# Linear-attention and gated-MLP block on one core: other queues for the first loads, a row-tiled spread of 1/den, and new instruction orders

## The chip, the core and the metric

The kernel runs on one core of a Trainium2 chip. The metric is the device time of one execution in microseconds (us); smaller is better. Three runs of the kernel before gave a median of 241.5 us, from 240.93 to 242.02. One more execution was profiled. Times inside the profile count from the start of its span.

## The reference

Two blocks follow each other on x, which has 2048 tokens and 512 features. All data is bf16.

```python
# A: linear attention, 32 heads of 16
q, k, v = split(layernorm(x) @ wqkv)
phi = lambda t: where(t > 0, t + 1, exp(t)) + 1e-6
pq, pk = phi(q), phi(k)
kv, z = einsum('bhsd,bhse->bhde', pk, v), einsum('bhsd->bhd', pk)
num, den = einsum('bhqd,bhde->bhqe', pq, kv), einsum('bhqd,bhd->bhq', pq, z) + 1e-6
h = x + merge_heads(num / den) @ wo
# B: gated MLP with a mix over tokens, Fh = 896
zz = gelu(layernorm(h) @ w_in)
z1, z2 = zz[..., :Fh], layernorm(zz[..., Fh:])
g = einsum('ts,bsf->btf', w_sp, z2) + b_sp
out = h + (z1 * g) @ w_out
```

## The kernel before, in words

Tokens are worked in 16 tiles of 128 (n = 0 to 15), which form 4 groups of 512 (gq or tg = 0 to 3). In the order of the work:

- **Loads** (L495, called from L507 to L520). The x tiles 0, 2 and 3 and then wq (the query weights) go out on SP's DMA queue, x tile 1 and then wk (the key weights, 512 KB) on ScalarE's. An x tile is 128 KB. SP goes on with the other x tiles.
- **First layernorm, per tile**: statistics on VectorE (L576, then L580, here "stats" and "aggr"), 1/sqrt of the variance on ScalarE as Ln and Exp (L590, L592) for tiles 0 to 3, then the normalisation on VectorE (L611, "norm"). Tiles 0 to 3 are transposed by TensorE (L645, "tr": four matmuls) and copied from PSUM by ScalarE (L652, "copy"); the others go through DMA transposes on SP's queue (L637).
- **Key projection** (L734, "k0" is that of tile 0, four matmuls) and its phi on ScalarE and VectorE (L711 to L720); products of keys and normalised x (L766); **query projection** (L748), which needs the transposes of all four tiles of its group.
- **The denominator**, for two groups of tokens at a time (`den`, L849): a matmul in four column strips (L858), Ln and Exp on ScalarE for the reciprocal (L863, L866), a spread over heads and features by matmuls with the 0/1 matrix `sel` (L874, four 128x128 matmuls per group, one PSUM bank), a copy on ScalarE per group (L878), and two multiplications of pq by it on VectorE per group (L882, each a half of the group's tokens).
- The product of kv and wo (L819, L829, L838, its copies L845 and L847), the attention output (L904, four matmuls per tile) added to x on VectorE (L909), the second layernorm (L576 again, L618), DMA transposes, then the two halves of the first MLP matmul (L939, L970), the token mix (L1009) and the last projection (L1027).

Ahead of the real work, and between its first pieces, TensorE runs matmuls on constants whose results nobody reads (L564, "dummies"). Eight stand at the start, two wait for the first stats, one for the first Exp; four short ones follow tr0 and tr1.

Nothing is scheduled at run time. Every operation of the program has a number, counted in the order in which the Python code makes it. `ORDER` lists the numbers; each engine executes its own operations in that order and waits on semaphores for what they need. An operation that waits holds up everything behind it on its engine. `SLOT` gives each PSUM or SBUF tile its place.

The order of `ORDER` at the start of the kernel before reads, engine by engine:

- SP: x0, x2, x3, wq, x4-5, ... ; ScalarE: x1, wk, table load, Ln0, Exp0, Ln2, Exp2, copy0, Ln1, Exp1, copy2, ...
- VectorE: stats0, aggr0, stats2, norm0, aggr2, stats1, norm2, aggr1, stats3, norm1, aggr3, norm3, ...
- TensorE: 8 + 2 dummies, tr0, 3 dummies, tr2, k0, tr1, k2, dummy, tr3, k1, dummy, k3, four query parts, ...

Of the kernel before, what the change touches and what calls it, by code (L numbers as in the profile page):

```python
# [7 lines left out]
ACT = mybir.ActivationFunctionType  # L8
ALU = mybir.AluOpType

P = 128
# [1 line left out]


ORDER = [
# [34 lines left out]
]  # L50
SLOT = [
# [6 lines left out]
]  # L58


# [294 lines left out]
def bass_sequential_preLN__linear_attn_block__mixer_gmlp__prompt_kernel(  # L355
# [11 lines left out]
    _, S, D = A_x.shape  # L367
# [3 lines left out]
    GW = 512  # L371
    NT, KD, KF, NG = S // P, D // P, FH // P, S // GW
    TPG = GW // P
# [101 lines left out]
    def bank(i):  # L475
        return lambda a: a[:, i, :]
# [10 lines left out]
    def act_c(n, ptr=0):  # L487
        return 0.07 + 0.000833 * n + 0.093 * ptr
# [18 lines left out]
        xl[a] = load(eng, f"x{a}", x[a:b, :], x_dram[a * P:b * P, :].rearrange("(n p) d -> p n d", p=P),  # L507
                     int((b - a) * P * D * 2 + more), bias, **kw)

    load_x("sp", 0, 1)  # L510
    load_x("act", 1, 2)
    load("act", "wk", wqkv[:, D:2 * D], w3[:, :, D:2 * D], D * D * 2)
    load_x("sp", 2, 3)
    load_x("sp", 3, 4)
    load("sp", "wq", wqkv[:, 0:D], w3[:, :, 0:D], D * D * 2)
    for a in (4, 6):
# [332 lines left out]
    def den(gs):  # L849
        n = len(gs)  # L850
        t = Tile(PS)
        pq = View(s_tq, (NG + gs[0]) * GB_, [n, KD, GW], BF16)

        def mm(e):
            for c in range(KD):
                for j in range(TPG):
                    o = t(bank(0)).ap()[CG * j:CG * (j + 1), 0:n * P].rearrange("p (g k) -> p g k", g=n)
                    i = e.matmul(o, lhsT=zb.ap[:, CG * c:CG * (c + 1)], rhs=pq.ap[:, :, c, j * P:(j + 1) * P],  # L858
                                 start=(c == 0), stop=(c == KD - 1), skip_group_check=True)
            return i  # L860
        op("pe", n * MM, mm, r=[zb.all(), pq.all()], w=[t()], mode=1)
        rr, rb = rr_v[gs[0]:gs[-1] + 1, :], rb_v[gs[0]:gs[-1] + 1, :]
        op("act", act_c(n * P, 1), lambda e: e.activation(  # L863
            flat(rr.ap()), t(bank(0)).ap()[:, 0:n * P], ACT.Ln, bias=eps[1:2].ap(), scale=1.0),
           r=[t(), eps[1:2]], w=[rr])
        last_lnexp.append(op("act", act_c(n * P), lambda e: e.activation(rb.ap(), rr.ap(), ACT.Exp, scale=-1.0),  # L866
                             r=[rr], w=[rb]))
        for gq in gs:
            t2 = Tile(PS)
            r1, rs = rb_v[gq, :], rs_v[gq, :]  # L870

            def sp_(e, t2=t2, r1=r1):
                for j in range(TPG):
                    k = e.matmul(t2(bank(0)).ap()[:, j * P:(j + 1) * P], lhsT=sel.ap[:, j * P:(j + 1) * P], rhs=r1.ap(),  # L874
                                 start=True, stop=True, skip_group_check=True)
                return k
            op("pe", 4 * MS, sp_, r=[sel.all(), r1], w=[t2()])
            op("act", act_c(GW), lambda e, t2=t2, rs=rs: e.activation(rs.ap(), t2(bank(0)).ap(), ACT.Copy), r=[t2()],  # L878
               w=[rs])
            for a in (0, GW // 2):  # L880
                d, m = pqT[gq][:, a:a + GW // 2], rs_v[gq, a:a + GW // 2]
                op("dve", dve_c(KD * GW // 2, 2), lambda e, d=d, m=m: e.tensor_tensor(  # L882
                    d.ap(), d.ap(), m.ap().rearrange("p (a f) -> p a f", a=1).to_broadcast([P, KD, GW // 2]),
                    ALU.mult), r=[d, m], w=[d])
# [202 lines left out]
```

## Time and profile before

| | |
|---|---|
| median of three runs | 241.5 us |
| profiled execution, its own time | 240.84 us |
| its span in the profile | 239.6 us |
| TensorE busy | 98% of the span |
| VectorE busy | 55% |
| ScalarE busy | 33% |

The profile lists what each engine did and when. A chain of waits is followed back from the last instruction: each piece of it is the work that the next piece waited for. A row of it has the start in us, the length in us, the engine, the tile and the line. In a timeline a matmul's length also has the time in which its result drains, so that consecutive matmuls overlap there; in the chain they don't. In a list of DMA issues the last number is the time from issue to landing.

### The profile page before, as it was taken

Reading aid. Unit: us, or ns where it says so; the run is one execution under the profiler, and the core shown is the slowest. Engines: PE = TensorE matmul, PEld = TensorE weight load, DVE = VectorE, ACT = ScalarE, POOL = GpSimd, SP = SyncE. Lnnn points to the kernel's source line nnn. Section 1 sums busy time; section 2 is a strip of 40 time slices with the busy share of each in tenths; the row PEclk is TensorE's granted clock in tenths of the full one; section 3 lists DMA queues with packets and bytes.
Section 4 is the critical chain, followed back from the end, with each engine's and each line's share of the span. In section 5 each row is a group of like instructions: output and inputs, shape, how many; then the busy total and the mean of one; then the engine's idle time right before and its main releaser. Section 6 shows DMA issues by size and latency. Waiting matters only on the chain.

```text
span 239.6 us, 3023 instructions
## 1 busy us (share of the span) xinstructions
PE 235.2 (98%) x1172; PEld 110.3 (46%) x1194; DVE 132.6 (55%) x269; ACT 79.2 (33%) x101; POOL 34.1 (14%) x84
## 2 busy tenths in 40 slices
PE   8999999999999999999999999999999999999996
PEld 2544444554444454544444444444444444444443
DVE  4898866389999934996233233341333513323444
ACT  3883844784666889654600000000000000000000
POOL 7114312001334600436000000000000000000000
DMA  6941349966232332594444544445000200000022
GB/s 205 320 88 26 74 101 266 351 101 138 71 68 44 68 66 59 130 208 89 91 106 93 88 107 95 102 105 117 0 0 0 68 23 0 0 3 0 0 87 88
DMA packets 56702, 21.83 MB, mean 91 GB/s; under 512 B 50704, under 2 KB 55824, under 8 KB 56688
## 3 DMA queue, kind: packets, MB, share of 16 engines
q1 hardware_dynamic: 54928, 16.62, 31.6%
q0 software_dynamic: 944, 4.33, 5.7%
q10 hardware_dynamic: 816, 0.70, 1.0%
q8 instruction: 9, 0.15, 0.3%
q14 instruction: 5, 0.04, 0.1%
HBM read 7.47 MB, written 2.10 MB: 40 GB/s over the span
## 4 chain that ended last, share of the span: by engine, by line
PE 96%; DMA 1%; issue 1%; DVE 1%; ACT 0%; ACTq 0%
PE ps L1009 40%; PE ps L1027 10%; PE ps L939 10%; PE ps L970 10%; PE ps L766 6%; PE ps L734 6%; PE ps L748 6%; PE ps L904 6%; DMA xh<-in_A_x_dram 1%; PE ps L645 1%; PE ps L858 0%; PE ps L838 0%; PE ps L782 0%; PE ps L874 0%; PE ps L819 0%
## 5 line engine op out<-in xcount | busy, mean ns | idle before, releaser
L1009 PE MATMUL ps<-wsp,pk_xn_z 128*128 128x512 bf16 x328 | 72.6, 379 | 0.4
L1016 DVE TENSOR_TENSOR e<-ps,e 128x512 bf16<-128x512 f32 x28 | 19.3, 691 | 68.1 <-PE ps L1009 68.1
L1009 PEld LDWEIGHTS ps<-wsp,pk_xn_z 128*128 128x128 bf16 x336 | 32.9, 98 | 39.6
L939 PE MATMUL ps<-win,hT 128*128 128x384 bf16 (+1 forms) x126 | 25.9, 352 | 0.1
L970 PE MATMUL ps<-hT,win 128*128 128x512 bf16 x109 | 25.6, 379 | 0.2
L1027 PE MATMUL ps<-wout,xT_pq_z 128*128 128x512 bf16 (+2 forms) x118 | 24.6, 366 | 0.1
L1009 PE MATMUL ps<-wqkv_wsp,pk_xn_z 128*128 128x512 bf16 x110 | 24.2, 379 | 0.1
L576 DVE BATCH_NORM_STATS2 small<-xh 128x6 f32<-128x512 bf16 x32 | 21.0, 676 | 3.5 <-DMA xh<-in_A_x_dram 3.4
L948 DVE BATCH_NORM_STATS2 small<-pk_xn_z 128x6 f32<-128x512 bf16 (+1 forms) x32 | 18.0, 605 | 7.4 <-ACT pk_xn_z L944 7.4
L711 ACT ACTIVATE e<-ps 128x1024 bf16<-128x1024 f32 x16 | 16.4, 1027 | 12.6 <-PE ps L734 8.6
L939 PEld LDWEIGHTS ps<-win,hT 128*128 128x128 bf16 x128 | 12.5, 98 | 12.6
L1027 PEld LDWEIGHTS ps<-wout,xT_pq_z 128*128 128x128 bf16 x119 | 11.5, 98 | 13.0
L1033 DVE TENSOR_TENSOR e<-ps,xh 128x512 bf16<-128x512 f32 (+2 forms) x17 | 11.2, 660 | 11.3 <-PE ps L1027 11.3
L1009 PEld LDWEIGHTS ps<-wqkv_wsp,pk_xn_z 128*128 128x128 bf16 x112 | 10.9, 98 | 13.2
L597 POOL TENSOR_TENSOR small<-small 128x2 f32<-128x2 f32 x22 | 16.6, 764 | 1.5
L970 PEld LDWEIGHTS ps<-hT,win 128*128 128x128 bf16 x112 | 10.9, 98 | 12.5 <-ACT xT_pq_z L975 0.3
L975 ACT ACTIVATE xT_pq_z<-ps 128x1024 bf16<-128x1024 f32 (+1 forms) x16 | 14.1, 917 | 7.5 <-PE ps L970 7.3
L944 ACT ACTIVATE pk_xn_z<-ps 128x896 bf16<-128x896 f32 x16 | 14.4, 916 | 5.7 <-PE ps L939 5.7
L734 PE MATMUL ps<-wqkv_wsp,xT_pq_z 128*128 128x512 bf16 x64 | 15.7, 379 | 0.0
L766 PE MATMUL ps<-pk_xn_z 128*128 128x512 bf16 x62 | 15.5, 379 | 0.2 <-issue 0.2
L748 PE MATMUL ps<-xT_pq_z,wqkv_wsp 128*128 128x512 bf16 x61 | 14.7, 379 | 0.2
L904 PE MATMUL ps<-pk_xn_z,xT_pq_z 128*128 128x512 bf16 x63 | 14.3, 379 | 0.2 <-issue 0.2
(71 smaller groups left out, 172.9 us busy)
## 6 DMA issues: line engine op xcount, KB each, us to landing
out_dram<-e SPq DMA_DIRECT2D x15, 128.0 KB, 1.7
win<-in_B_w_in_dram POOLq DMA_DIRECT2D x1, 1792.0 KB, 9.9
xh<-in_A_x_dram SPq DMA_DIRECT2D x4, 256.0 KB, 6.1
wout<-in_B_w_out_dram POOLq DMA_DIRECT2D x1, 896.0 KB, 6.3
wsp<-in_B_w_sp_dram SPq DMA_TRANSPOSE x48, 2.9
wqkv_wsp<-in_A_wqkv_dram ACTq DMA_DIRECT2D x1, 512.0 KB, 4.9
wqkv_wsp<-in_A_wqkv_dram SPq DMA_DIRECT2D x1, 512.0 KB, 5.6
xh<-in_A_x_dram SPq DMA_DIRECT2D x1, 512.0 KB, 7.2
```

The source lines that it names most:

```text
L576: op("dve", dve_c(512), lambda e: e.bn_stats(s6.ap(), src.ap()), r=[src], w=[s6])
L597: return op("pool", 0.665, lambda e: e.tensor_tensor(dst.ap(), dst.ap(), h.ap(), ALU.pow), r=[dst, h], w=[dst])
L734: i = e.matmul(t(bank(ti)).ap(), lhsT=lhs.ap()[:, c, :], rhs=rhs.ap()[:, c, :], start=(c == 0), stop=(c == KD - 1))
L748: r_ = e.matmul(t(bank(i)).ap(), lhsT=lhs.ap()[:, c, :], rhs=rhs.ap()[:, c, :], start=(c == 0), stop=(c == KD - 1))
L766: r = e.matmul(txk[h](bank(i)).ap(), lhsT=xx.ap()[:, c * P:(c + 1) * P], rhs=kk.ap(), start=(n == 0), stop=(n == NT - 1))
L904: i = e.matmul(t(bank(ti)).ap(), lhsT=l.ap()[:, c, :], rhs=mw[c, :].ap(), start=(c == 0), stop=(c == KD - 1))
L939: k = e.matmul(t(bank(i)).ap()[:, 0:b - a], lhsT=l.ap()[:, c, :], rhs=win[c, a:b].ap(), start=(c == 0), stop=(c == KD - 1))
L948: op("dve", dve_c(b - a), lambda e, s6=s6, src=src: e.bn_stats(s6.ap(), src.ap()), r=[src], w=[s6])
L970: k = e.matmul(t(bank(i)).ap(), lhsT=l.ap()[:, c, :], rhs=r_.ap()[:, c, :], start=(c == 0), stop=(c == KD - 1))
L1009: k = e.matmul(t(bank(0)).ap(), lhsT=l.ap()[:, s - a, :], rhs=r_.ap()[:, s - a, :], start=(s == 0), stop=(s == NT - 1))
L1016: op("dve", dve_c(512), lambda e: e.tensor_tensor(gb().ap(), t(bank(0)).ap(), bsp().ap()[:, tg * GW:(tg + 1) * GW], ALU.add), r=[t(), bsp( ...
L1027: k = e.matmul(t(bank(0)).ap()[:, 0:b - a], lhsT=l.ap()[:, fc, :], rhs=wout[fc, a:b].ap(), start=(fc == 0), stop=(fc == KF - 1))
```

## The change

Four things change.

1. x tile 0 is loaded in two halves of 256 columns, one issued by SP and one by ScalarE. Tiles 1 and 2 follow on ScalarE's queue. wk goes out on SP's queue, second there, ahead of x3 and wq.
2. The spread of 1/den takes one operation for a pair of groups. For each j of 0 to 3 it multiplies only the 32 rows of `sel` and of the reciprocals that matter (rows 32j to 32j+31) and 256 columns, each j into a bank of its own: four matmuls for two groups where there were eight.
3. The copies after it take two banks each and are cut by halves of the tokens (a = 0, 1) in place of groups. The multiplications L882 stay as they were.
4. `ORDER` and `SLOT` are new. The numbers in the new `ORDER` are shifted by one from the second load on.

```diff
 ORDER = [
-    0, 3, 4, 5, 27, 28, 13, 24, 15, 11, 18, 19, 1, 2, 26, 35, 36, 12, 14, 29, 30, 31, 32, 37, 38, 21, 33, 20, 25, 22,
-    23, 49, 39, 50, 34, 123, 124, 40, 125, 126, 127, 51, 42, 6, 7, 8, 9, 10, 52, 41, 53, 43, 17, 56, 44, 54, 45, 46,
...
+    28, 29, 0, 3, 5, 6, 7, 8, 1, 36, 30, 31, 32, 33, 34, 35, 124, 125, 17, 9, 2, 4, 27, 10, 11, 22, 23, 25, 14, 15, 12,
+    24, 16, 19, 13, 26, 43, 37, 44, 20, 38, 21, 50, 39, 40, 45, 46, 51, 47, 52, 126, 41, 127, 53, 42, 48, 54, 128, 129,
...
-    load_x("sp", 0, 1)
+    for i, (eng, a, b) in enumerate((("sp", 0, D // 2), ("act", D // 2, D))):
+        load(eng, f"x0{'ab'[i]}", x[0, a:b], x_dram[0:P, a:b], P * D, BIG)
     load_x("act", 1, 2)
-    load("act", "wk", wqkv[:, D:2 * D], w3[:, :, D:2 * D], D * D * 2)
-    load_x("sp", 2, 3)
+    load("sp", "wk", wqkv[:, D:2 * D], w3[:, :, D:2 * D], D * D * 2)
+    load_x("act", 2, 3)
     load_x("sp", 3, 4)
...
+        t2 = [Tile(PS, 2), Tile(PS, 2)]
+        r1 = rb_v[gs[0]:gs[-1] + 1, :]
+        def spread(e):
+            for j in range(TPG):
+                q = slice(CG * j, CG * (j + 1))
+                k = e.matmul(t2[j // 2](bank(j % 2)).ap()[:, 0:n * P], lhsT=sel.ap[q, j * P:(j + 1) * P], rhs=r1.ap()[q],
+                             start=True, stop=True, skip_group_check=True)
+            return k
+        op("pe", MM * n / TPG, spread, r=[sel.all(), r1], w=[t2[0](), t2[1]()], mode=2)
+        for a in range(2):
+            rs = rs_v[gs[0]:gs[-1] + 1, a * GW // 2:(a + 1) * GW // 2]
+            op("act", act_c(GW), lambda e, t2=t2, rs=rs, a=a: e.activation(
+                rs.ap().rearrange("p g (j t) -> p j g t", j=2),
+                t2[a]().ap()[:, :, 0:n * P].rearrange("p j (g t) -> p j g t", g=n),
+                ACT.Copy), r=[t2[a]()], w=[rs])
         for gq in gs:
-            t2 = Tile(PS)
-            r1, rs = rb_v[gq, :], rs_v[gq, :]
-            def sp_(e, t2=t2, r1=r1):
-                for j in range(TPG):
-                    k = e.matmul(t2(bank(0)).ap()[:, j * P:(j + 1) * P], lhsT=sel.ap[:, j * P:(j + 1) * P], rhs=r1.ap(),
-                                 start=True, stop=True, skip_group_check=True)
-                return k
-            op("pe", 4 * MS, sp_, r=[sel.all(), r1], w=[t2()])
-            op("act", act_c(GW), lambda e, t2=t2, rs=rs: e.activation(rs.ap(), t2(bank(0)).ap(), ACT.Copy), r=[t2()],
-               w=[rs])
```

Read by engine, the new lists say:

- SP: x0 left half, wk, x3, wq, x4-5, ... ; ScalarE: x0 right half, x1, x2, table load, Ln0, Exp0, Ln1, Exp1, Ln2, Exp2, copy0, copy1, Ln3, Exp3, copy2, copy3, ...
- VectorE: stats0, stats1, aggr0, aggr1, stats2, norm0, aggr2, norm1, norm2, stats3, aggr3, norm3, ... (36, 43, 37, 44, 50, 40, 51, 47, 54, ... in the new numbers)
- TensorE: 8 + 2 + 1 dummies, tr0, dummy, tr1, 3 dummies, tr2, k0, k1, tr3, k2, three query parts, k3, the fourth, ... No dummy stands behind k0.
- Later, TensorE: the last two query parts, then L904 for tiles 0, 1, 2, 3, 6, L858 for groups 2 and 3, L904 for tile 4, the spread of groups 2 and 3, tiles 5, 7, 14, 8, 9, 15 and 10 to 13. VectorE multiplies group 0's tokens of tiles 0 and 1 (L882) right after the copy L847. In the kernel before, L904 began with tile 2, and two tiles (6 and 7) stood between L858 and the spread.
- The mix and the last projection keep their order; three L970 blocks move in between the first pieces of the mix.

76 rows, old and new, of tables (ORDER, SLOT) are left out of this document.

## The prediction

> **What bounds the kernel now.** The page comes first, for the share of each engine, then the chain of waits in order of time.
>
> ```profile
> span 239.6 us, 3023 instructions
> PE 235.2 (98%) x1172; PEld 110.3 (46%) x1194; DVE 132.6 (55%) x269; ACT 79.2 (33%) x101; POOL 34.1 (14%) x84
> ```
>
> ```profile
> 3.45 0.71 DVE small L576
> ...
> 4.17 0.19 DVE small L580
> ...
> 5.51 0.61 PE ps L645 x4
> 6.12 0.61 PE ps L564 x3
> 6.73 0.27 PE ps L645 x4
> 7.01 0.86 PE ps L734 x4
> ...
> 9.08 0.22 PE ps L645 x4
> ...
> 10.28 0.86 PE ps L734 x4
> 11.14 0.43 PE ps L748 x2
> ...
> 44.29 0.55 PE ps L858 x16
> ...
> 46.67 0.45 PE ps L874 x8
> ...
> 50.60 0.99 PE ps L838 x16
> 51.59 1.85 PE ps L748 x8
> ...
> 56.90 0.55 PE ps L858 x16
> ...
> 226.01 11.63 PE ps L1027 x60
> ```
>
> From 5.51 us to 237.64 (226.01 + 11.63) TensorE is the chain without a break worth naming. So the time is the start of TensorE's real work, plus its work, plus a tail that the change leaves alone. Three things can move it: when the real work begins and whether it runs on from there; how much TensorE work there is; and stalls that the new orders bring where there are none. The profiled execution took 240.84 us, 1.24 more than its span and 0.66 less than the median of 241.5. The sum is made on 240.84 and its difference is then put on the median.
>
> **The front: a yardstick.** At 11.14 TensorE has done four tr and four k. After the change, by the orders, tr0 to tr2 and all dummies stand ahead of k0; then k0, k1, tr3, k2 and k3 can run back to back with query parts between them. That is four times 0.86 and one tr of 0.22, 3.66 us from the start K of k0. The front gains if K lies before 11.14 - 3.66 = 7.48, counted as the chain counts.
>
> **The front: the loads.** Here are the issues and their landings: tile 0 on SP and tile 1 on ScalarE, then wk on ScalarE, tile 2 on SP, then tile 3 on SP. Two rows of timelines give the issue times, and the last row is all that DMA queues moved from 3.66 to 4.70 us (q10 is ScalarE's queue).
>
> ```profile
> xh<-in_A_x_dram SPq DMA_DIRECT2D x1, 128.0 KB, 2.6
> xh<-in_A_x_dram ACTq DMA_DIRECT2D x1, 128.0 KB, 2.8
> ```
> ```profile
> wqkv_wsp<-in_A_wqkv_dram ACTq DMA_DIRECT2D x1, 512.0 KB, 4.9
> xh<-in_A_x_dram SPq DMA_DIRECT2D x1, 128.0 KB, 2.7
> ```
> ```profile
> xh<-in_A_x_dram SPq DMA_DIRECT2D x1, 128.0 KB, 4.4
> ```
> ```profile
> 0.80 1.33 SPq L495 DMA_DIRECT2D xh<-in_A_x_dram  x3
> ```
> ```profile
> 1.24 0.46 ACTq L495 DMA_DIRECT2D wqkv_wsp<-in_A_wqkv_dram  x1
> ```
> ```profile
> DMA packets 321, 0.33 MB, mean 316 GB/s; under 512 B 0, under 2 KB 321, under 8 KB 321
> ...
> q10 hardware_dynamic: 321, 0.33, 92.2%
> ```
>
> SP's first three issues took 1.33 us together, so they stand some 0.45 apart: 0.80, 1.24, 1.70. Tile 1 landed at 0.80 + 2.8 = 3.6, tile 2 at 1.24 + 2.7 = 3.9, wk at 1.24 + 4.9 = 6.1, tile 3 at 1.70 + 4.4, also 6.1. Tile 3 is the telling one. It was issued on another queue than wk, half a microsecond later, and waited for it: for over 1 us nothing but wk's packets moved. The two queues therefore do not share the rate evenly. A small load issued after wk lands after wk, whichever queue it is on.
>
> The change puts wk second on SP, at 1.24, and tile 1 second on ScalarE, at about the same time; tile 2 comes third, at about 1.70, surely behind wk. Whether tile 1 goes ahead of wk is open. I take the case that wk goes first, since tile 2 and wk were issued together before, at 1.24, and SP's was through first: tile 2 landed at 3.9, while more than half of wk moved after 3.66. Then tile 1 is the end of 768 KB where tile 3 was the end of 1024. At 316 GB/s the 256 KB between are 0.83 us, so tile 1 lands at about 5.3 and tile 2, 0.4 later, at 5.7. Bounds: 3.6 (as before) and 6.1 (as tile 3 before).
>
> The Trainium skill has a rule that would soften this ("DMA: Bandwidth & Descriptors", Queues, rings and completion order): each DMA engine alternates between the queues it has work for, after a packet of typically 9 to 17 descriptors. Tile 1 would then slip in after half of wk, and by an estimate from the rate above land near 4.7. The row of 321 packets, more than half of wk's 512 and with none of SP's among them, speaks against so early a turn.
>
> **The front: who waits for tile 1.** This is what decides. The new VectorE order is stats0, stats1, aggr0, aggr1, stats2, norm0. VectorE executes in order, so aggr0, with tile 0 long ready, stands behind stats1 and its wait for tile 1; and norm0 stands behind stats2. Splitting tile 0 in halves then gains nothing. The steps by the old distances between starts:
>
> ```profile
> 4.17 0.18 DVE L580 BATCH_NORM_AGGREGATE small<-small 128x2 f32<-128x6 f32 x1
> 4.27 0.66 DVE L576 BATCH_NORM_STATS2 small<-xh 128x6 f32<-128x512 bf16 x1
> 5.02 0.43 DVE L611 TENSOR_SCALAR pk_xn_z<-xh,small 128x512 bf16<-128x512 bf16 x1
> 5.38 0.16 DVE L580 BATCH_NORM_AGGREGATE small<-small 128x2 f32<-128x6 f32 x1
> 5.46 0.65 DVE L576 BATCH_NORM_STATS2 small<-xh 128x6 f32<-128x512 bf16 x1
> 6.14 0.41 DVE L611 TENSOR_SCALAR pk_xn_z<-xh,small 128x512 bf16<-128x512 bf16 x1
> ```
> ```profile
> 5.57 0.29 ACT L590 ACTIVATE small<-small 128x1 f32<-128x1 f32 x1 [0.58 <-DVE small L580]
> 5.90 0.20 ACT L592 ACTIVATE small<-small 128x1 f32<-128x1 f32 x1
> 6.16 0.60 ACT L652 ACTIVATE xT_pq_z<-ps 128x512 bf16<-128x512 bf16 x1
> ```
>
> stats1 starts at 5.33; aggr0 0.72 later (3.45 to 4.17), at 6.05; aggr1 0.10 later, stats2 at 6.25 (tile 2 is there); norm0 0.68 later (5.46 to 6.14), at 6.93. aggr2 follows 0.36 later (5.02 to 5.38), at 7.29. Ln2 comes 0.20 after aggr2 (5.38 to 5.57), at 7.49, Exp2 0.33 later at 7.82, norm2 0.24 later (5.90 to 6.14), at 8.06. copy0 stands behind Exp2 on ScalarE and starts at 8.05; tr2 starts 0.49 after norm2 (5.02 to 5.51) and takes 0.22, so TensorE is free for k0 at 8.77, and copy0's 0.60 is over by 8.65. The chain counts a piece up to 0.17 later than the timeline (k0: 7.01 against 6.84 when its first matmul starts). So **K = 8.94**, and the front costs 8.94 - 7.48 = 1.46 us. wk itself (6.1 before, now earlier in the line) is there long before k0. Tile 3 and wq have the same bytes ahead of them as before, and their readers come later. The table load on ScalarE moves by one DMA issue of 0.46 and hides in the wait for Ln0 at 6.25; if tile 1 came at 3.6 it would still be done before Ln0. GpSimd makes its constants in another order, and their first reader, Ln0, comes later too.
>
> **The spread.** Two sets of eight 128x128 matmuls, 0.45 us each (46.67), become two sets of four on 32 rows and 256 columns. The rows of before have no row-tiled matmul. The nearest is L858, tiled in four column strips: 16 matmuls of 256 columns, at 0.108 (half of 0.86 / 4) 1.73 us one by one, took 0.55, so four ran at once, with 0.12 over. By that a set of four takes 0.11 + 0.12 = 0.23, and two sets save 0.44. Bounds: four at once without the 0.12, 0.11 a set, saves 0.68; one by one, 0.55 a set, costs 0.20. I take 0.44. The copies keep their number and size (512 elements each); they lie beside TensorE.
>
> The skill has the same drain as a rule ("TensorEngine Tiling (Array Packing)", Key Properties): a change of tiling mode drains TensorE. Without the drain the sum would be 0.24 lower; the 0.12 in L858 agrees with the rule.
>
> **The new orders behind the front.** TensorE has no wait to lose, so they can only add. Two places are short of cover.
>
> ```profile
> 51.66 1.22 DVE L847 CAST pk_xn_z<-ps 128x1024 bf16<-128x1024 f32 x1
> 52.79 0.68 DVE L882 TENSOR_TENSOR xT_pq_z<-xT_pq_z,wsp 128x1024 bf16<-128x1024 bf16 x1
> ```
> ```profile
> 57.50 0.47 ACT L863 ACTIVATE wsp<-ps,small 128x256 f32<-128x256 f32 x1 [2.08 <-PE ps L858]
> 58.01 0.42 ACT L866 ACTIVATE wsp<-wsp 128x256 bf16<-128x256 f32 x1
> ```
>
> First, L904 now begins with tile 0, which needs the L882 that follows L847. That ended at 53.47 (52.79 + 0.68), while TensorE was free at 53.44 (51.59 + 1.85): a stall of about 0.1 with the hop. Second, from the end of L858 (57.45) to the end of L866 (58.43) are 0.98 us. One L904 tile (0.86) now covers them, where two did: about 0.15. Behind it VectorE's order L909, L882, L909 leaves each L882 some 0.1 of slack by the same rows; a slip there costs up to 0.5. I take 0.25 for all, with 0 and 1.0 as bounds.
>
> **The sum**: +1.46 - 0.44 + 0.25 = +1.27. 240.84 becomes 242.1; on the median, 241.5 becomes **242.8 us**, slower by 0.5%.
>
> **The rivals.**
>
> *Tile 1 goes ahead of wk.* It then lands near 3.7 and stats1 starts at 4.17, but tile 2 still lands behind wk, at 5.7, and norm0 stands behind stats2: norm0 6.41, Exp2 7.30, copy0 7.53, norm2 7.54, k0 at 8.25 + 0.17 = 8.42, the front +0.94. 242.3 us. For it: ScalarE's two issues are short. Against it: SP's turn above.
>
> *Not slower: the loads share after all.* If wk gives way to tiles 1 and 2, so that they land by 4.1 and 4.9, stats1 starts 0.72 after stats0 at 3.45, at 4.17, and K is 8.94 - 1.16 = 7.78; with tile 0's halves 0.3 earlier, 7.5. The front is then 0 to +0.30 and the spread decides: 241.3 to 241.6. The point from which it decides is tile 1 at 4.1, tile 2 at 5.0. Against it: tile 3 before.
>
> *TensorE stays at half pace.* Ten dummies before tr0 went at half pace, and so did tr0:
>
> ```profile
> 0.83 4.42 PE L564 MATMUL ps<-const-bfloat16-1.0 128*128 128x512 bf16 x10 [0.83 <-PEq L1072]
> ```
>
> 0.43 each against 0.22 (0.86 / 4) for later ones of that size. The full pace came after 5.5 us of nearly unbroken dummies. In my forecast they end at 5.3 and the next waits for Exp0, until about 6.6. If the pace is not reached ahead of tr0, three tr at 0.43 and four dummies at 0.21 put k0 at 7.42 + 2.14 + 0.17 = 9.73: 0.8 more, 243.6. The skill's rule ("TensorE: Matmul & The Clock Gate", Part 1) is a free-running window of some 3.4 us that has to be busy; this trace shows one transition only and can't date the window.
>
> *The spread isn't tiled.* The four run one by one: +0.20 in place of -0.44, 243.4.
>
> **How the numbers follow.** The forecast has 0.34, tile 1 ahead of wk 0.24, sharing 0.24, half pace 0.13, the spread untiled 0.05. A difference of 0.5% is about what a measurement of this kernel can tell from no change: above 242.7 is slower, under 240.3 faster. Half pace, the spread and most of the forecast are slower, 0.46. The second case, sharing and the forecast's lower part are the same, 0.46; the low end of sharing with the best spread (0.24 more) and no stall (0.25 more) comes near faster, 0.08. The range runs from 240.8, sharing with those two, to 243.7, half pace.
>
> **What would show it.** Right: stats1 starts after 5 us, released by a DMA, and aggr0 behind it; tr0 begins near 7.4; k0 to k3 have no dummy between them; each spread takes 0.23 in the chain and small waits stand ahead of the first L904 and of the second spread. Wrong: stats1 directly behind stats0; a row of DMA packets in which both queues move while wk is under way; or a wait of TensorE over 0.5 us behind the front, which I have not priced.

## The result and the profile after

The changed kernel takes 245.3 us (median of six executions, 243.86 to 245.72), the kernel before in the same measurement 241.5 (240.91 to 242.02): a ratio of 1.016, 95% interval 1.0137 to 1.0182. It is slower by 3.8 us, where the prediction had 1.3 and a range that ended at 243.7. The profiled execution took 245.30 us, 4.46 more than that of before.

The first two lines of the page, after:

```profile
span 244.0 us, 3008 instructions
PE 237.7 (97%) x1163; PEld 110.7 (45%) x1186; DVE 132.5 (54%) x269; ACT 79.1 (32%) x101; POOL 35.5 (15%) x84
```

TensorE is busy for 2.5 us more than before, with nine instructions fewer. So part of the loss is not waiting: the same work went slower. The chain of waits, after (start, length, what; the lines of the file are shifted: L577 is stats, L612 norm, L646 tr, L565 the dummies, L735 the key projection, L749 the query projection, L859 the denominator, L875 the spread, L910 the attention output):

```profile
1.72 5.08 DMA xh<-in_A_x_dram
...
6.82 0.69 DVE small L577
7.51 0.31 DVE pk_xn_z L612
7.83 0.10 DVE small L581
...
7.97 0.58 PE ps L646 x4
...
8.77 0.43 PE ps L646 x4
...
9.84 0.43 PE ps L646 x4
10.26 3.37 PE ps L735 x8
13.63 0.22 PE ps L646 x4
13.85 0.86 PE ps L735 x4
...
51.14 0.22 PE ps L875 x4
51.36 0.99 PE ps L749 x4
...
63.79 0.29 PE ps L875 x4
64.08 5.29 PE ps L910 x24
...
238.68 3.43 PE ps L1033 x22
```

Three things are to be seen. The chain now begins with the load of tile 2, issued at 1.72 and landed at 6.80, where it began with tile 0. K, the start of k0, is 10.26. And k0 and k1 took 3.37 together, 1.69 each, where a key projection takes 0.86 (the row at 13.85): TensorE ran at half pace until the end of k1, and tr0 to tr2 went at 0.43 and more, not 0.22.

The account by the prediction's yardstick: before, four tr and four k were done at 11.14. After, k0 and k1 (3.37), tr3 (0.22), k2 and k3 (twice 0.86) from 10.26 on make 15.57. The front is 4.43 us later, and the last matmul ends at 242.11 where it ended at 237.64: 4.47 later. **The whole loss is in the front, by 13.63 us, where k1 ends.** All that is behind it, spread and new orders together, comes to nothing.

The timeline of the front, after (in brackets the idle time ahead and what ended it):

```profile
3.03 0.69 DVE L577 BATCH_NORM_STATS2 small<-xh 128x6 f32<-128x512 bf16 x1 [3.03 <-DMA xh<-in_A_x_dram]
5.77 0.69 DVE L577 BATCH_NORM_STATS2 small<-xh 128x6 f32<-128x512 bf16 x1 [2.04 <-DMA xh<-in_A_x_dram]
6.38 0.30 DVE L581 BATCH_NORM_AGGREGATE small<-small 128x2 f32<-128x6 f32 x2
...
7.22 0.61 PE L565 MATMUL ps<-const-bfloat16-1.0 128*128 128x512 bf16 x1 [1.97 <-ACT small L593]
```

Tile 0's halves let stats0 start at 3.03 (3.45 before), and nothing comes of it: stats1 waits for tile 1 until 5.77, aggr0 behind it starts at 6.38, and TensorE stands idle for 1.97 us. The load lists, from issue to landing, for the two issued at 1.24 and for the two at 1.70:

```profile
wqkv_wsp<-in_A_wqkv_dram SPq DMA_DIRECT2D x1, 512.0 KB, 4.8
xh<-in_A_x_dram ACTq DMA_DIRECT2D x1, 128.0 KB, 4.5
```
```profile
xh<-in_A_x_dram SPq DMA_DIRECT2D x1, 128.0 KB, 4.9
xh<-in_A_x_dram ACTq DMA_DIRECT2D x1, 128.0 KB, 5.1
```

Tile 1 needed 4.5 us where before it needed 2.8; tile 2 needed 5.1 where it needed 2.7.

### The profile page after: what moved, and what is told of

It is laid out like the page before. It is cut to its first block, busy times and chain, and to the rows that moved or that the text cites. A ratio compares the mean times of both kernels' runs of the same rounds, so it can differ in the third digit from the quotient of the medians.

```text
span 244.0 us, 3008 instructions
## 1 busy us (share of the span) xinstructions
PE 237.7 (97%) x1163; PEld 110.7 (45%) x1186; DVE 132.5 (54%) x269; ACT 79.1 (32%) x101; POOL 35.5 (15%) x84
## 4 chain that ended last, share of the span: by engine, by line
PE 95%; DMA 2%; issue 1%; DVE 1%; ACT 0%; ACTq 0%
PE ps L1015 39%; PE ps L945 10%; PE ps L1033 10%; PE ps L976 10%; PE ps L735 6%; PE ps L749 6%; PE ps L767 6%; PE ps L910 5%; DMA xh<-in_A_x_dram 2%; PE ps L646 1%; PE ps L859 0%; PE ps L839 0%; PE ps L783 0%; PE ps L820 0%; ACTq L495 0%
## 5 line engine op out<-in xcount | busy, mean ns | idle before, releaser
L945 PE MATMUL ps<-win,hT 128*128 128x512 bf16 (+1 forms) x127 | 25.5, 352 | 0.1
L577 DVE BATCH_NORM_STATS2 small<-xh 128x6 f32<-128x512 bf16 x32 | 21.0, 677 | 5.2 <-DMA xh<-in_A_x_dram 5.1
L1033 PEld LDWEIGHTS ps<-wout,xT_pq_z 128*128 128x128 bf16 x119 | 11.5, 98 | 13.0
L735 PE MATMUL ps<-wqkv_wsp,xT_pq_z 128*128 128x512 bf16 x63 | 17.2, 410 | 0.1
L749 PE MATMUL ps<-xT_pq_z,wqkv_wsp 128*128 128x512 bf16 x61 | 14.9, 380 | 0.2
L910 PE MATMUL ps<-pk_xn_z,xT_pq_z 128*128 128x512 bf16 x62 | 14.2, 379 | 0.1
```

Source lines behind the costliest of these rows:

```text
L577: op("dve", dve_c(512), lambda e: e.bn_stats(s6.ap(), src.ap()), r=[src], w=[s6])
L735: i = e.matmul(t(bank(ti)).ap(), lhsT=lhs.ap()[:, c, :], rhs=rhs.ap()[:, c, :], start=(c == 0), stop=(c == KD - 1))
L749: r_ = e.matmul(t(bank(i)).ap(), lhsT=lhs.ap()[:, c, :], rhs=rhs.ap()[:, c, :], start=(c == 0), stop=(c == KD - 1))
L910: i = e.matmul(t(bank(ti)).ap(), lhsT=l.ap()[:, c, :], rhs=mw[c, :].ap(), start=(c == 0), stop=(c == KD - 1))
L945: k = e.matmul(t(bank(i)).ap()[:, 0:b - a], lhsT=l.ap()[:, c, :], rhs=win[c, a:b].ap(), start=(c == 0), stop=(c == KD - 1))
L1033: k = e.matmul(t(bank(0)).ap()[:, 0:b - a], lhsT=l.ap()[:, fc, :], rhs=wout[fc, a:b].ap(), start=(fc == 0), stop=(fc == KF - 1))
```

## The experiments

The kernel before was measured again beside each experiment, with medians from 240.85 to 241.23 us, where it had 241.5 beside the change. Where two kernels of different measurements are compared, the difference by the ratios to the kernel before stands beside that of the medians. In the diffs, `...` marks lines left out.

**1 and 2. wk behind the small tiles.** Two kernels undo the place of wk and keep all else of the change: once wk goes last on ScalarE and tile 2 to SP, once wk stays on SP but third. The numbers of the first loads in `ORDER` follow the issues.

```diff
     load_x("act", 1, 2)
-    load("sp", "wk", wqkv[:, D:2 * D], w3[:, :, D:2 * D], D * D * 2)
-    load_x("act", 2, 3)
+    load("act", "wk", wqkv[:, D:2 * D], w3[:, :, D:2 * D], D * D * 2)
+    load_x("sp", 2, 3)
```
```diff
     load_x("act", 1, 2)
+    load_x("sp", 2, 3)
     load("sp", "wk", wqkv[:, D:2 * D], w3[:, :, D:2 * D], D * D * 2)
-    load_x("act", 2, 3)
```

> The changed kernel with its new orders, the halves of x tile 0 and the row-tiled spread, but wk back on ScalarE behind tile 1, and tile 2 back on SP. Theory (the front: wk goes ahead of tiles 1 and 2, VectorE's order hands their lateness to tile 0, and TensorE falls back to half pace in the gap): tile 1 lands by 3.6 us, stats1 starts near 3.7, k0 near 7.3 at full pace, so the front costs nothing and the time is 241.3 us (240.8 to 241.8), the spread giving some 0.4 and two small stalls taking 0.3. Rival (the new orders cost it, in the stages behind the front too): over 244.

> As wk_last, but wk is on SP's queue, third there, behind tile 2 and ahead of tile 3. If the order of issue decides, tiles 1 and 2 land as early as in wk_last (by 3.6 and 4.0) and the time is the same, 241.3 us within 0.4. If SP's queue is served before ScalarE's, tile 1 on ScalarE still lands behind wk, over 4.7, and the time is 243 or more.

Measured: 240.94 us for the first, ratio 1.0003 (0.9994 to 1.0013), and 240.91 for the second, 1.0006 (0.9996 to 1.0017). All of the loss is gone in both. The chain of the first:

```profile
1.23 2.94 DMA xh<-in_A_x_dram
...
4.19 0.69 DVE small L578
...
7.59 1.73 PE ps L736 x8
```

Tile 1 lands at 4.17, k0 starts at 7.59, and k0 and k1 take 1.73: full pace. So the place of wk among the issues is the cause, not the queue that carries it. (Both kernels also move tile 2 to SP, which was not tried by itself; tile 1 keeps its queue and its place, and lands at 4.17 and 4.01 where it landed at 5.74.) These kernels have the row-tiled spread and the new orders too, and come out level with before: those parts of the change together neither gain nor lose by more than 0.4 us.

**3. The half pace by itself.** The loads of the change stay; the two dummies that wait for stats0 become ten (five matmuls each), so that TensorE has something to do while tiles 1 and 2 are awaited. The helper `keep_busy` gets an argument for the number of matmuls, and in experiment 4 one for their columns.

```diff
...
-            keep_busy(n, cost, [], [gate] if gate.eng != "pe" else [])
+            keep_busy(n, cost, [], [gate] if gate.eng != "pe" else [], 5 if gate is first[0] else 1)
```

> The changed kernel, with each of the two dummies that wait for the first stats made five, so that TensorE is busy until about 7 us. Theory with half pace as a cost of its own: tr0 to k3 run at full pace, k0 starts near 9.4 in place of 10.26, and 2.3 us of the front's 4.4 come back: 243.0 us (242.5 to 243.5). Rival (all is lateness of the data): 245.3, no change.

Measured: 243.07 us, ratio 1.009 (1.0076 to 1.0104). Its chain:

```profile
1.71 5.25 DMA xh<-in_A_x_dram
...
9.54 1.73 PE ps L739 x8
```

Tile 2 is as late as in the change (6.96), but k0 and k1 go at full pace. More matmuls on constants made the kernel some 2 us faster: 2.2 by the medians, 1.7 by the ratios, 2.3 by the spans of the two profiles (244.0 and 241.7). The loss of the change is therefore two losses of about the same size: some 2 us that the late tiles cost (K at 9.54 against 7.59 and 7.44 in experiments 1 and 2), and some 2 us that the idle TensorE cost.

**4. The half pace put into the kernel before.** The reverse: old loads and orders, but the last four of the eight warming dummies and the two behind stats0 are cut to four columns.

```diff
-        warm = [keep_busy(512, MM, warm)]
+        warm = [keep_busy(512, MM, warm, cols=0 if i < 4 else 4)]
...
+            keep_busy(n, cost, [], [gate] if gate.eng != "pe" else [], cols=4 if gate is first[0] else 0)
```

> The kernel before, with one thing changed: the last four of the eight warming dummies and the two dummies ahead of tr0 are cut from 512 to 4 columns, so that TensorE is idle from about 2.6 us to tr0 at 5.5 us, with the old loads and orders. Theory (the half pace of the changed kernel's front comes from TensorE's idle time ahead of tr0, and nothing else in the change brings it): tr0 still starts at 5.5 us, but the transposes take 0.43 us and k0, k1 1.7 us each until about 11 us; some 2 us are lost, 243.0 us (242.4 to 243.8). Rival (the idle time costs nothing by itself, the late loads are all): within 0.3 us of before, 240.9 to 241.5.

Measured: 242.6 us, ratio 1.0065 (1.0044 to 1.0086); 1.7 us lost with every load in its old place. The rival, that idle time costs nothing by itself, falls. The chain:

```profile
5.39 0.60 PE ps L649 x4
...
7.28 1.71 PE ps L738 x4
...
9.41 1.71 PE ps L738 x4
```

tr0 starts as before (5.39 against 5.51), and then the first two key projections take 1.71 each; the next two take 0.86 again.

**5. VectorE's order.** The prediction had said that aggr0 and norm0, queued behind stats1 and stats2, decide. Here aggr0, Ln0, Exp0 and norm0 go ahead of stats1, with the loads of the change; once as that alone, once with 24 short matmuls behind tr0 that keep TensorE busy.

```diff
+ORDER = [i for i in ORDER if i not in (37, 38, 39, 40)]
+ORDER[ORDER.index(43):ORDER.index(43)] = [37, 38, 39, 40]
```

> The changed kernel with four operations moved in its order: aggr0, Ln0, Exp0 and norm0 stand ahead of stats1. The loads stay. Theory (the late tiles 1 and 2 still hold k0, since tr1 and tr2 stand ahead of k0 on TensorE; the VectorE order alone was not the cause, it only ties tile 0 to them): norm0 comes 2 to 3 us earlier, tr0 too, but k0 starts at most 0.5 us earlier; 244.8 us (244.0 to 245.3). Rival (the prediction's reading: VectorE's queue is what ties k0 to the late tile, so that freeing it gives the front back): 243 us or under.

> The changed kernel with aggr0, Ln0, Exp0 and norm0 ahead of stats1, and with the first dummy behind tr0 made 24 matmuls of 256 columns (2.6 us), so that TensorE does not stand idle while tiles 1 and 2 are awaited. Beside the kernel that only has more dummies (243.1 us, k0 at 9.5) it tells what the order of VectorE alone is worth at full pace. Theory (k0 stands behind tr2 on TensorE, and tr2 needs tile 2, which lands near 7 us whatever VectorE does first; all that is saved is norm0's 0.3 us between stats2 and aggr2): full pace, k0 at 9.0 to 9.4 us, 242.8 us (242.4 to 243.1). Rival (the prediction's reading, that VectorE's queue is what ties tile 0 to the late tiles and decides the start of k0): k0 back near 7.5 to 8 us, 241.5 us or under.

Measured: 245.51 us for the first, ratio 1.0171 (1.0143 to 1.0199), no gain on the change. This execution shows the clock itself. TensorE in stretches of half a microsecond (length, busy time and count, granted clock, share of the DMA engines, GB/s):

```profile
7.00:7.50 0.50, 0.00 (x0) 1.00 1.11 348
7.50:8.00 0.50, 0.00 (x0) 0.64 1.10 346
8.00:8.50 0.50, 0.03 (x1) 0.50 1.10 346
...
14.00:14.50 0.50, 0.50 (x2) 0.54 0.00 0
```

tr0 ran early, at 5.34, then TensorE had nothing until 8.47. The granted clock fell to 0.50 during that idle time, at about 7.6, and came back only near 14.5, after 6 us of unbroken work. Moving work forward without closing the hole behind it just moved the hole.

The second took 244.03 us, ratio 1.0102 (1.0064 to 1.0139), and missed my 242.4 to 243.1. Its chain:

```profile
1.72 6.07 DMA xh<-in_A_x_dram
...
10.24 1.67 PE ps L741 x7
```

Full pace, but tile 2 landed at 7.78 in this execution, 0.8 later than in experiment 3 with the same loads. The row has seven of the eight matmuls of k0 and k1; the eighth is missing from the trace. Counted back from their end at 11.91, with 1.73 for the eight, k0 started at 10.18, which is 0.64 later than there. From tile 2's landing to k0 are 2.40 us here and 2.58 there. So the VectorE order is worth about 0.2 us; the rival (k0 near 7.5 to 8) falls. The rest of its excess over experiment 3 lies later, where the chain leaves TensorE for a transpose by DMA; I did not follow that up.

**6. k0 ahead of the late tiles, on every engine.** With tr1 and tr2 ahead of k0, TensorE's order ties k0 to them as well. Here tile 0 goes through to k0 before stats1, tr1 and tr2: once with the loads of the change, once with wk third on SP.

```diff
+FRONT = [37, 38, 39, 40, 126, 41, 127, 128, 42, 131]
+ORDER = [i for i in ORDER if i not in FRONT]
+ORDER[ORDER.index(43):ORDER.index(43)] = FRONT
...
+SLOT[0] = 7
```

> The changed kernel with its loads as they are (wk ahead of tiles 1 and 2), but tile 0 is taken through to k0 ahead of tile 1 on every engine: aggr0, Ln0, Exp0, norm0, tr0, two dummies, copy0 and k0 stand ahead of stats1. Theory (the loads cost nothing until something that could go on stands behind a late tile; with k0 ahead of tr1 and tr2 TensorE works from 5.4 us on, idles at most 1 to 2 us, and the clock is not taken back for long): k0 starts when wk has landed, at 6.0 to 6.5 us, at full pace; tr1 follows near 8 us; 242.0 us (241.3 to 243.3), 2 to 4 us under the changed kernel. Rival (the loss is the late bytes themselves, in whatever order they are used): 244 us or more.

> The changed kernel with wk issued third on SP, behind tiles 1 and 2 (tile 0 in halves, tile 1 on ScalarE, tile 2 on SP), and k0 ahead of stats1, tr1 and tr2 on every engine. Theory (what is left in the front is the wait for wk, which lands at 6.1 us; k0 can start there, and all that follows is ready in time): k0 at 6.2 to 6.5 us, k3 done at 10.3 to 10.7 us where before it was 11.1; 240.4 us (240.0 to 240.8), faster than both kernels by 0.2% against before. Rival (TensorE is idle ahead of k0 and pays for it with the clock, or tile 1 and 2 now come late because norm0 goes first): 241 us or more.

Measured: 242.83 us for the first, ratio 1.0076 (1.0062 to 1.009), under the change by 2.5 us (2.0 by the ratios). In its timeline k0 starts at 6.58, at full pace:

```profile
6.58 1.02 PE L739 MATMUL ps<-wqkv_wsp,xT_pq_z 128*128 128x512 bf16 x4 [0.55 <-ACT xT_pq_z L657]
```

Yet k2 ends at 12.39 (its chain: 11.53 + 0.86), as in experiment 3, where it ends at 12.35 (9.54 + 1.73 + 0.22 + 0.86). What came off is the half pace; the 2 us of the late tiles are still there, only behind k0. My expectation of 242.0 was 0.8 too low, though inside its range, and what I had as the rival, that the late bytes cost their time in whatever order they are used, is right for this half of the loss.

The second took 241.7 us, ratio 1.0028 (1.0017 to 1.0038), slower than wk third alone, and refutes my 240.4. Its chain:

```profile
5.17 0.61 DVE small L582
...
5.99 0.59 DVE small L582
...
7.38 0.41 DVE pk_xn_z L617
7.79 0.61 DVE small L582
...
10.15 0.86 PE ps L740 x4
```

Now VectorE is the chain, with short steps of ScalarE between: with norm0 ahead, the later tiles' statistics and normalisations run one behind the other from 5.17 on, and k2 ends at 11.02, where with wk third alone it would end at 7.44 + 2.81 = 10.25. With the tiles in time the change's own order was the better one.

**7. Tile by tile.** All four tiles of the first group one behind the other on every engine, with the loads of the change; one list of 38 numbers put into `ORDER` behind stats0, and six entries of `SLOT`.

```diff
+FRONT = [36, 124, 125, 37, 38, 39, 40, 126, 41, 42, 127, 128, 131, 43, 44, 45, 46, 47, 48, 49, 129, 130, 132, 50, 51, 52,
+         53, 54, 55, 56, 140, 57, 58, 59, 60, 61, 62, 63, 141]
+ORDER = [i for i in ORDER if i not in FRONT]
+ORDER[ORDER.index(26) + 1:ORDER.index(26) + 1] = FRONT
```

> The changed kernel with its late loads, but the first four tiles are worked one behind the other on every engine: stats0, aggr0, norm0, then tile 1, and so on; TensorE runs tr0, k0, tr1, k1 and so on. Theory (the VectorE order hands tile 1's lateness to tile 0): tr0 starts near 5.1 and k0 near 6.3, as soon as wk is there, and k3 ends near 11.5 in place of 15.6, so 241.5 to 242.5 us. Rival (the late loads alone cost it, in any order): over 244.

Measured: 246.88 us, ratio 1.0249 (1.0219 to 1.0279). The expectation failed, for a reason of its own:

```profile
9.17 1.04 PE ps L740 x4
...
10.47 0.61 ACT xT_pq_z L658
...
11.12 1.04 PE ps L740 x4
```

Each key projection waits for a copy of its own tile that nothing covers, 1.95 us from one to the next. Behind the front TensorE then stands idle once more, for 2.23 us until 19.79, and the granted clock falls to 0.50 from about 20.2 to 23.6; a key projection at 21.26 takes 1.71. It is no test of the VectorE order.

**8. The parts that were to gain, in the kernel before.** The kernel before with tile 0 in halves only; and that with the row-tiled spread and its copies as well, in the old order (four places in `SLOT` for the wider tiles).

```diff
-    load_x("sp", 0, 1)
+    for i, (eng, a, b) in enumerate((("sp", 0, D // 2), ("act", D // 2, D))):
+        load(eng, f"x0{'ab'[i]}", x[0, a:b], x_dram[0:P, a:b], P * D, BIG)
```

> The kernel before with only tile 0's load split in two column halves, one on SP and one on ScalarE; the other loads keep their queues and places, the orders are the old ones. Theory (the halves land earlier, and with the old orders VectorE can use that): tile 0 is there 0.4 to 0.5 us earlier; stats0, aggr0, norm0 and tr0 come forward until tile 1 or the ScalarE steps bind: 240.5 us (240.2 to 240.9), 0.2 to 0.5 under before. Rival (ScalarE's extra issue pushes tile 1 and wk back by 0.46 us, and k0 waits for wk or norm1 as long as it gained): no change, 240.8 to 241.5.

> As the kernel with only tile 0's halves, and the row-tiled spread in place of the eight small matmuls a set, in the old order. Theory (the spread saves 0.22 us a set in its own row, but the matmuls next to it take some 0.12 longer, as a change of mode is paid on the way in and on the way out): 0.1 to 0.25 us less than the kernel with the halves alone. Rival 1 (the prediction's step): 0.44 less. Rival 2 (GW-wide copies that cover two groups come later than the old ones and the second set waits): the same or 0.2 more.

Measured: 240.71 us with the halves, ratio 0.9991 (0.9981 to 1.0001); 241.51 with halves and spread, 1.0025 (1.001 to 1.004). Tile 0 does land 0.43 earlier, at 2.99, but of that 0.14 is left when k3 is done (11.00 against 11.14): VectorE is the chain there from norm0 to norm2, and norm0 took 0.66 where it took 0.44 before. The interval still holds 1. The chain of the second:

```profile
48.11 0.22 PE ps L875 x4
48.33 0.99 PE ps L749 x4
...
60.62 0.25 PE ps L875 x4
...
60.89 0.61 ACT wsp L881
...
61.55 7.08 PE ps L910 x32
```

The spread itself takes the predicted 0.22, but the four matmuls after it take 0.99, where the same four take 0.86 behind the old spread. The net gain is 0.10 a set. At the second set, with tiles of two banks in the places that I gave them, the next attention output was to use banks that the spread still held: TensorE waits 0.68 us for the copy (60.87 to 61.55), and the gain is lost several times over. My first expectation missed because of that wait, which the old tiles of one bank each don't have; the second rival there had this cause, but at 0.2 us. The medians of the two kernels lie 0.8 apart, and not all of that is the spread: the profiled execution, the slowest of twelve (242.86), also had wk land at 8.1 (1.7 + 6.4) where the halves alone had it at 6.2 (1.7 + 4.5), so that k3 was done at 12.58 and not at 11.00. How much of such a delay the median of 241.5 holds is open; the rows of the spread hold none of it.

No version here beats the kernel before by more than its measurement can tell; the halves alone come nearest.

## Why the prediction was wrong, point by point

- **The sign and the cause were right**: wk, second on SP, holds back tiles 1 and 2, and without that the rest of the change costs nothing that could be measured (experiments 1 and 2).
- **Tile 1's landing** was put at 5.3 by the rate of 316 GB/s and a wk that goes through first. It was 5.74 (1.24 + 4.5), for other reasons: it even landed ahead of wk (1.24 + 4.8 = 6.04), against "a small load issued after wk lands after wk", so that 5.3 came near by luck. Two answers on the DMA traffic after, from 2.7 to 3 and from 3 to 4 us (q1 is SP's queue), show a slow beginning, and one from 4 to 5 shows both queues moving:

```profile
DMA packets 8, 0.01 MB, mean 27 GB/s; under 512 B 0, under 2 KB 8, under 8 KB 8
```
```profile
DMA packets 132, 0.14 MB, mean 135 GB/s; under 512 B 0, under 2 KB 132, under 8 KB 132
```
```profile
q1 hardware_dynamic: 252, 0.26, 73.8%
q10 hardware_dynamic: 124, 0.11, 32.9%
```

  Before, these first 1.3 us carried 0.31 MB, after 0.15. Why wk starts so slowly is open. Then the queues share about two to one, and not by the strict precedence that I had read out of tile 3. This is nearer to the Trainium skill's rule that each DMA engine takes its queues in turn ("DMA: Bandwidth & Descriptors", Queues, rings and completion order). By that rule I had given an estimate of 4.7; the slow start is not in it, and the landing was later than by either reading.
- **Tile 2's landing** was put at 5.7, 0.4 behind tile 1. It was 6.80, beside tile 3 at 6.6 (1.70 + 4.9). But stats1 from 5.77 lets stats2 start at 6.69 at the earliest, so this added only 0.13. Together the two landings make K later by 0.57: 9.51, and experiment 3 has 9.54 at full pace. **The waits were mis-sized by 0.6 us.**
- **The step that failed is the half pace.** I wrote that the dummies "end at 5.3 and the next waits for Exp0, until about 6.6", and then made it a rival with 0.13 and 0.8 us. But the forecast has this idle time in itself, and its sum has nothing for the pace behind it. The idle time was 1.97 us; whether the forecast's 1.3 would have done it is not shown: the longest gap in these fronts that kept full pace is 0.91 us (experiment 6, first kernel, until 8.52), and behind those of 1.97 (the change), 2.23 (experiment 7) and 2.64 us (experiment 5) TensorE went at half pace. And the rival was priced for the tr and dummies ahead of k0 only. After, those took 0.75 us more (10.26 against 9.51), and k0 and k1 another 1.65 (3.37 against 1.72): 2.40, over half of the 4.43. The terms are 1.46 + 0.57 + 2.40 = 4.43.
- **"This is what decides"**, of VectorE's order, was wrong. With aggr0 and norm0 freed (experiment 5) K moves by 0.2, and with k0 freed as well (experiment 6) the end of k2 hardly moves (12.39 against 12.35). Tiles 1 and 2 are needed for the next work anyway.
- **The spread** was to save 0.44 and saves about 0.1. The 0.12 of drain stands once in my sum, inside the tiled set; it is paid a second time by the matmuls behind it (0.99 for 0.86 at 51.36). A row of the chain of before says so, behind L858:

```profile
44.84 0.97 PE ps L766 x4
```

  Those are four matmuls, which take 0.86 elsewhere. The second set takes 0.29, its followers 0.11 more (5.29 for 24, 5.18 at 0.216 each), and it waits 0.1 for Exp: nothing gained there. The Trainium skill has the drain on a change of mode ("TensorEngine Tiling (Array Packing)", Key Properties); these rows agree, and add that it counts in both directions.
- **The stalls** of the new orders, 0.25, come out at some 0.15: with the spread's 0.1 they net to nothing, in the change (4.47 against 4.43) and in experiment 2, whose span is 239.6, that of before.

## What to carry to other kernels

Issue what the first work needs ahead of the large load that is needed later, on whichever queue: here wk, issued at 1.24 and not at 1.70, moved tile 1, a 128 KB load, by 1.7 us (5.74 against 4.01). Price an idle gap of TensorE in its warm-up twice, once for the wait and once for the matmuls at half pace behind it, and if the wait can't go, fill it with matmuls on constants. A gain of a few tenths inside a row is real only when the row after it is read too.

## What was not expected of the hardware

- Behind a pause of TensorE, full pace came late: after some 6.1 us of work in the kernel before with the gap (from 5.39 to about 11.5), 6.0 in experiment 5 (8.47 to 14.5) and 6.2 in the change (7.22 to about 13.4), but 3.8 in experiment 7 (19.79 to 23.6). In the last the clock was down for 3.4 us (20.2 to 23.6), in experiment 5 for 6.8 (7.6 to 14.5). The mean granted clock agrees: these two executions have 0.993 and 0.986, and among those of the change one took 245.72 us at 0.986 and two took 243.9 at 0.993. At half clock 0.014 x 244.5 / 0.5 are 6.8 us, and 0.007 are 3.4. The Trainium skill's free-running window of some 3.4 us ("TensorE: Matmul & The Clock Gate", Part 1) fits both, as one window and two, and fits a return after 3.4 to 6.8 us of work.
- The clock record of the profiled change says 1.00 throughout the front, though its matmuls took 0.43; that of the kernel before says 1.00 for the ten dummies at 0.43 as well. Whether full pace had come and gone in the change, or had not yet come when TensorE paused, this record can't say. The durations are the surer sign.
- Five executions with the loads of the change had tile 2 at 6.80, 6.96, 7.18, 7.23 and 7.78 us. A load in a crowd lands later and less surely; what share this has in the scatter of these kernels' times, 0.4 to 1.9 us between the fastest and the slowest execution, was not tried.
